# Linear attention and a feed-forward layer on one core: k read from its staging buffer, key-value products of two batches together, row squares summed through ScalarE's accumulator

## The chip, the cores and the metric

The kernel runs on one core of a Trainium2 chip. The metric is the device time of one execution in microseconds. Lower is better.

The core has a matrix engine (TensorE, "PE" in the profile; its weight loads are "PEld"), a vector engine (VectorE, "DVE"), an activation engine (ScalarE, "ACT"), GpSimd ("POOL") and SyncE ("SP"). Each works through its own instructions in order. Here POOL and SP do little but issue transfers (DMA).

## The reference

```python
kv  = einsum('bhsd,bhse->bhde', k, v)          # 8 batches, 8 heads, 576 rows, 64 columns
out = einsum('bhsd,bhde->bhse', q, kv)
rms = sqrt(mean(out * out, axis=-1) + 1e-06)   # over the 64 columns of a head
x   = out / rms * g_norm                       # then [4608 tokens, 512], heads side by side
h   = x @ w_in                                 # 512 -> 2048
g   = maximum(h, 0) + alpha * minimum(h, 0)
y   = g @ w_out                                # 2048 -> 512
```

The inputs and the result are float32; the kernel computes in fp16 and accumulates in float32.

## The kernel before

**Windows, stages, units.** The 4608 tokens are cut into nine windows of 512. Stage w does three things at once: the first feed-forward product of window w, the second product of window w-1, and the attention of window w+1, which makes the input of the next stage. A stage has 16 units (`u`). The instructions of every engine stand in the order in which the code writes them; there is no planner.

**A unit.** `m1_group(w, g)` runs four matmuls of 128x512 (L507) into a PSUM bank `h_ps`. From stage 2 on there are two such banks, taken in turn. ScalarE computes `m_sb` = relu(-h) from the bank (L514), and VectorE then `gt` = h + beta * m_sb (L518), after which the bank is free. Then come seven matmuls of 128x256 for the second product of the window before (L688). That product is done with seven block products instead of eight; the sums that this needs are VectorE's (`s_sum`, L623 to L629). Finished parts are read out by ScalarE (`p1` in unit 2, `c11` in unit 7) or by VectorE (`u2`, `u3`, `c22`, `c21`, `c12`) and stored by DMAs of POOL and SP. In unit 0 of stages 3 and up the first matmul group is split (`late`): 384 columns first, the last 128 columns after four of the seven other matmuls (L530), since these columns of the input are the last to arrive.

**Attention of windows 3 and up** ("rows" form, `attention(w + 1, u)`). `row_kv(b)` makes the key-value products of one batch, head by head: 40 matmuls of 64 columns (L1001) into a PSUM tile, two ScalarE copies from there into `kv_masked` (L1007). `rows_mm` makes the outputs of four blocks of 128 tokens (L452), token by row, eight heads of 64 columns next to each other. For each block i: `rows_sq` squares 512 columns on ScalarE (L463), `rows_ssq` sums each head's 64 squares on VectorE (L469), `rows_rs` makes the reciprocal root of eight numbers per row on ScalarE (L479), `rows_norm` multiplies on VectorE (L487) and has SP issue a DMA transpose of the block into `xt` (L492), the input of the next stage. `ROW_AT` says in which unit each step stands. From window 4 on: kv in unit 0, both `rows_mm` in unit 1, the squares of blocks 0 to 3 in units 1, 3, 5, 7, the sums in 2, 4, 7, 9, root and norm in 3, 6, 8, 11. Window 3 (`W_ROW`, handled in stage 2) has a schedule of its own, up to unit 12.

**Loads.** At the start of stage w, `load_gated(w + 2)` puts the loads of batch w+2 on POOL's queue: the last 64 rows of q, k, v (`load_rem`, into `qsb`, `ksb`, `vsb`) and the first 512 rows (`load_main` into the staging buffers `kst` and `vst`, two of each; `load_q` in four parts). POOL issues them in order, together with most stores; its first load of a stage waits for the last transpose of the q before. q is transposed by DMAs on SP's queue (`dma_t`). v is read where it was staged. k is first regrouped from `kst` (head, tile, column) into `ksb` (tile, head, column): for batches 4 to 7 by four ScalarE copies (`regroup_pair`, L195) in units 9, 11, 13 and 15 of stage w, for batch 3 by two ScalarE copies and one VectorE copy in unit 0 of stage 2. There are three `ksb`/`vsb` buffers (`NBUF`) and two `kv_masked` tiles.

Of the kernel before, what the change touches and what calls it, by code (L numbers as in the profile page):

```python
# [17 lines left out]
def kernel(  # L18
# [11 lines left out]
    nc = tc.nc  # L30
# [41 lines left out]
    def row_tile(shape, name):  # L72
        if not row_pool:
            early.close()
            row_pool.append(
                ctx.enter_context(tc.tile_pool(name="psr", bufs=2, space=bass.MemoryType.PSUM))
            )
        t = row_pool[0].tile([P, 2, W], FP32, name=name, tag="r")
        n = 1
        for x in shape:  # L80
            n *= x
        flat = t[:].rearrange("p b n -> p (b n)")[:, 0:n]
        names = [f"x{i}" for i in range(len(shape))]
        return flat.rearrange(
            f"p ({' '.join(names)}) -> p {' '.join(names)}", **dict(zip(names, shape))
        )
# [78 lines left out]
    def load_main(b, nm, h0=0, h1=H):  # L165
        if (b, nm) not in stages:
            stages[b, nm] = stage_p.tile([P, H, TPP, D], FP16, name=f"{nm}st", tag=f"{nm}st")
        nc.gpsimd.dma_start(
            out=stages[b, nm][:, h0:h1].rearrange("p h t d -> p h (t d)"),
            in_=srcs[nm][b, h0:h1, 0:MAIN, :].rearrange("h (p t) d -> p h (t d)", t=TPP),  # L170
        )
# [13 lines left out]
    def load_rem(b, nm):  # L185
        nc.gpsimd.dma_start(
            out=buf_of(b, nm)[0:REM, 0 if nm == "v" else TPP, :, :],
            in_=srcs[nm][b, :, MAIN:S, :].rearrange("h s d -> s h d"),
        )

    def regroup(b, nm, h0, h1, eng=None):
        dst = buf_of(b, nm)[:, 0:TPP, h0:h1, :].rearrange("p t h d -> p h t d")
        src = stages[b, nm][:, h0:h1, :, :]
        if eng is nc.scalar:
            nc.scalar.copy(out=dst, in_=src)  # L195
        else:
            (eng or nc.vector).tensor_copy(out=dst, in_=src)
# [6 lines left out]
    def load_gated(b):  # L204
        load_rem(b, "q")
        if b == B_NAT:
            load_q(b)
        load_rem(b, "k")
        load_main(b, "k")
        if b > B_NAT:  # L210
            load_q(b)
        load_rem(b, "v")
        load_main(b, "v")

    def regroup0(nm, j, n=1):
        i, h = divmod(2 * j, HH)
# [1 line left out]
            out=bufs[0][nm][0:P0, :, 2 * j : 2 * (j + n), :].rearrange("p t h d -> p h t d"),  # L218
            in_=stages[0, nm, i][0:P0, h : h + 2 * n],
        )  # L220

    def regroup_pair(b, nm, j):
        regroup(b, nm, 2 * j, 2 * j + 2, nc.scalar)


    WQ = 4
    w_in_sb = []
# [72 lines left out]


    qts, kvs, xts = {}, {}, {}
    kv_masked = [const_p.tile([P, NPAIR, P], FP16, name=f"kv_masked{i}") for i in range(2)]

    def rows(b):
        return P0 if b == 0 else P
# [60 lines left out]
    def step_kv(b, j, pool=(ps_s, "s")):  # L367
        ks, vs = pair_cols(b, "k", j), pair_cols(b, "v", j)
        kv_ps = pool[0].tile([P, P], FP32, name="kv_ps", tag=pool[1])
        for t in range(n_runs(b)):  # L370
            nc.tensor.matmul(  # L371
                out=kv_ps[:],
                lhsT=ks(t),
                rhs=vs(t),
                start=(t == 0),
                stop=(t == n_runs(b) - 1),
            )
        kvs[b, j] = kv_masked[b % 2][:, j, :]
        nc.vector.tensor_mul(out=kvs[b, j], in0=kv_ps[:], in1=mask32[:])


# [78 lines left out]
    def rows_sq(w, i):  # L460
        o_ps = ots.pop((w, "r", i))
        sq = attn_p.tile([P, 2, NPAIR, D], FP16, name="sq_sb")
        nc.scalar.activation(out=sq[:], in_=o_ps, func=AF.Square)  # L463
        ots[w, "r", i] = (o_ps, sq)

    def rows_ssq(w, i):
        o_ps, sq = ots.pop((w, "r", i))
        ssq = attn_p.tile([P, 2, NPAIR], FP32, name="ssq_r")
        nc.vector.tensor_reduce(  # L469
            out=ssq[:].rearrange("p h j -> p (h j)"),  # L470
            in_=sq[:].rearrange("p h j d -> p (h j) d"),
            axis=mybir.AxisListType.X, op=ALU.add,
        )
        ots[w, "r", i] = (o_ps, ssq)
# [516 lines left out]
            ATT_1.setdefault(at, []).append((what, j))  # L991
    ATT = {"t": step_t, "kv": step_kv, "ot": step_ot, "ssq": step_ssq}

    def row_kv(b):
        kv_ps = row_tile([NPAIR, D], "kv_ps")
        for j in range(NPAIR):
            ks, vs = pair_cols(b, "k", j), pair_cols(b, "v", j)
            for t in range(n_runs(b)):
                for i in range(2):
                    rows_i = slice(i * D, (i + 1) * D)  # L1000
                    nc.tensor.matmul(  # L1001
                        out=kv_ps[rows_i, j, :], lhsT=ks(t)[:, i, :], rhs=vs(t)[:, i, :],
                        start=(t == 0), stop=(t == n_runs(b) - 1), skip_group_check=True,
                    )
        for i in range(2):
            rows_i = slice(i * D, (i + 1) * D)
            nc.scalar.copy(out=kv_masked[b % 2][rows_i, :, rows_i], in_=kv_ps[rows_i, :, :])  # L1007
        for j in range(NPAIR):
            kvs[b, j] = kv_masked[b % 2][:, j, :]

    ATT_ROW = {}
    ROW_AT = {
        True: dict(
# [1 line left out]
            rs=(5, 7, 9, 12), norm=(5, 7, 9, 12),  # L1015
        ),
        False: dict(
            kv=(0,), mm=(1, None, 1, None), sq=(1, 3, 5, 7), ssq=(2, 4, 7, 9),
            rs=(3, 6, 8, 11), norm=(3, 6, 8, 11),
        ),  # L1020
    }
# [10 lines left out]
    def attention(w, u):  # L1032
        if W_ROW <= w < NW:
            for what, j in ATT_ROW[w == W_ROW].get(u, ()):
                if what != "kv":
                    ROWS[what](w, j)
                elif w < B:
                    row_kv(w)
            if w + 1 < B:
                dma_t(w + 1, QT_AT[w == W_ROW].get(u, ()))  # L1040
        elif w < NW:
            for what, j in (ATT_1 if w == 2 else ATT_AT).get(u, ()):
                if what == "t" and w >= B_NAT:
                    continue
                if w < B or what in ("ot", "ssq"):
                    if w == 2 and what in ("kv", "ssq"):
                        pool = Q_POOL if j % 2 == 0 else S_POOL
                        (step_kv if what == "kv" else step_ssq)(w, j, pool)
                    else:
                        ATT[what](w, j)  # L1050

    REG_AT = {9 + 2 * j: (("k", j),) for j in range(NPAIR)}

    Y3_AT = [(13, 13), (13, 13), (13, 13), (13, 14), (14, 14), (14, 15), (15, 15), (15, 15), (15, 15), (15, 15), (15, 15), (15, 15), (15, 15), (15, 15), (15, 16), (16, 16)]

    for w in range(1, NW):
        if w + 2 < B:
            load_gated(w + 2)
        for u in range(NF):
            if w >= W_ROW - 1 and u in R_FIRST:  # L1060
                y_read(w - 1, R_FIRST[u])
            late = w >= W_ROW and u == 0
            if late:
                h_ps = h_bank()
                m1_cols(h_ps, w, G_ORDER[u], 0, W - P)
            else:
                m1_group(w, G_ORDER[u])
            if w < 3 and (w, u) in ((1, NF - 1), (2, 0)):
                s_sum(1, w, 2)
            if w == W_ROW - 1:  # L1070
                scale_w_in(G_ORDER[u])
            if w > 1:
                unit_sums(w, u)
            if w == 1 and u == 1:
                regroup(2, "k", 0, H)
            if w == 2 and u == 0:
                h_tags[0] = ("h1", "h2")
                h_turn[0] = 0
            if w > 2 and u == 0 and not late:
                y_read(w - 2, "c12")  # L1080
            if w == 1:
                for i in range(*Y3_AT[u]):
                    y_mm(ys[3], 0, 3, i)
                    if i == NF - 1:
                        y_out(ys[3], 0, 3)
            else:
                for i in range(u * PER, (u + 1) * PER):
                    prod_mm(w - 1, *Y_LIST[i])
                    if late and i == 3:
                        m1_cols(h_ps, w, G_ORDER[u], W - P, W)  # L1090
                        y_read(w - 2, "c12")
                        m1_evac(h_ps, w, G_ORDER[u])
                for what in (R_ROW if w >= W_ROW - 1 else Y_READS).get(u, ()):
                    y_read(w - 1, what)
            attention(w + 1, u)
            if w == 1 and u == 12:
                dma_t(3, (3, 4, 0, 1, 2))
            if w == 1:
                for k in {5: (0,), 7: (1,)}.get(u, ()):
                    s_sum(1, 1, k)  # L1100
                    s_sum(1, 2, k)
            if w + 2 < B:
                for nm, j in REG_AT.get(u, ()) if w > 1 else ():
                    regroup_pair(w + 2, nm, j)
            if w == 2:
                if u == 0:
                    regroup_pair(3, "k", 0)
                    regroup_pair(3, "k", 1)
                    regroup(3, "k", HH, H)
    w = NW - 1  # L1110
    store_engines[0] = (nc.sync, nc.scalar)
    Y_READS[13] = Y_READS.pop(14)
# [54 lines left out]
```

## Time and profile before

| | us |
|---|---|
| median of 3 runs | 274.97 (273.76 to 275.08) |
| the profiled execution | 275.59 |
| its span, first to last instruction | 273.6 |

| engine | busy us | share of the span |
|---|---|---|
| PE | 266.3 | 97% |
| DVE | 227.9 | 83% |
| ACT | 155.9 | 57% |
| POOL | 86.2 | 32% |

Stage 2 begins at about 67 us in the trace, stage 3 at 94.5, stage 4 at 122, stage 5 at 149.8, stage 6 at 177; stage 8 ends at about 258, and what is left is the second product of the last window.

How to read it: a line of groups gives the line of code, the engine, the operation, what is written and read, the shapes and the count, then the busy time in us and the mean length of one in ns, then the engine's idle time before these instructions and what ended it. A timeline line gives the start and the length in us; the bracket at its end is the idle time of that engine just before. Matmuls are pipelined, so the lengths of successive ones overlap and their ends are modelled; the spacing of their starts is what counts. A DMA line gives the size in KB and the us from issue to landing. The engine that is busy all the time sets the end; the idle time of another one costs nothing by itself.

### The profile page before, as it was taken

The numbers are of one execution on the slowest core, as the hardware profiler recorded it, in microseconds if no ns is written. First come the engines' busy times: TensorE is split into PE (matmuls) and PEld (weight loads), VectorE is DVE, ScalarE is ACT, GpSimd is POOL, SyncE is SP. The second block draws the span as 40 slices with busy tenths as digits, with TensorE's granted clock in tenths as the row PEclk, the third lists the DMA queues.
The fourth block names the chain that finished last, engine by engine and source line by source line (L and its number), as shares of the span: only waits on it lengthen the run. The fifth ranks groups of instructions, "written<-read, shape, count | busy, mean of one in ns | idle before, by whom it ended". The sixth has DMA issues, their size and how long they took to land.

```text
span 273.6 us, 5687 instructions
## 1 busy us (share of the span) xinstructions
PE 266.3 (97%) x2181; PEld 170.8 (62%) x2181; DVE 227.9 (83%) x432; ACT 155.9 (57%) x294; POOL 86.2 (32%) x123
## 2 busy tenths in 40 slices
PE   7799999999999999999999999999999999999995
PEld 2364464555666766666666666666666666666794
DVE  6459938899889979997999799979998999877863
ACT  3267555879989865645565556555544553443210
POOL 8773462780733355226421551100110012000200
PEclk9799999999999999999999999999999999999999
DMA  8999999999999689966996699720222122201223
GB/s 161 196 200 199 197 202 189 220 112 162 137 164 180 99 129 149 170 153 113 155 167 147 112 156 164 151 89 19 77 60 77 22 77 60 77 1 41 77 79 116
DMA packets 87343, 34.56 MB, mean 126 GB/s; under 512 B 58884, under 2 KB 85652, under 8 KB 87316
## 3 DMA queue, kind: packets, MB, share of 16 engines
q0 software_dynamic: 58064, 24.35, 69.5%
q1 hardware_dynamic: 28212, 8.83, 17.1%
q10 hardware_dynamic: 1040, 1.02, 1.2%
q8 instruction: 17, 0.28, 0.4%
q14 instruction: 10, 0.08, 0.1%
HBM read 36.71 MB, written 9.44 MB: 169 GB/s over the span
## 4 chain that ended last, share of the span: by engine, by line
PE 95%; DMA 2%; DVE 1%; issue 0%; ACT 0%; POOLq 0%
PE h_ps L507 43%; PE yY L688 15%; PE yX L688 10%; PE yZ L688 10%; PE y L539 5%; DMA vst<-in_v_dram 2%; PE h_ps L530 2%; PE kv_ps L371 2%; PE or_ps L452 1%; PE kv_ps L1001 1%; PE ssq_ps L416 1%; PE qt_ps L327 1%; PE ot_ps L393 1%; PE yZ L683 1%; PE warm_ps L295 0%
## 5 line engine op out<-in xcount | busy, mean ns | idle before, releaser
L507 PE MATMUL h_ps<-xt,w_in_sb 128*128 128x512 f16 x544 | 136.9, 379 | 0.0
L514 ACT ACTIVATE m_sb<-h_ps 128x512 f32<-128x512 f32 x144 | 86.1, 599 | 78.1 <-PE h_ps L507 67.7
L518 DVE SCALAR_TENSOR_TENSOR gt<-m_sb,beta_sb,h_ps 128x512 f16<-128x512 f32 x144 | 106.2, 744 | 24.1 <-ACT m_sb L514 22.5
L507 PEld LDWEIGHTS <-w_in_sb 128*128 128x128 f16 x544 | 52.1, 98 | 40.0
L550 POOL DMA_DIRECT2D out_dram<-y_sb x36 | 22.6, 630 | 134.3 <-ACT y_sb L726 53.4
L688 PEld LDWEIGHTS <-s 128*128 128x128 f16 x496 | 48.5, 98 | 19.1
L688 PEld LDWEIGHTS <-gt 128*128 128x128 f16 x384 | 37.3, 98 | 14.0
L688 PE MATMUL yY<-wsum,s 128*128 128x256 f16 x256 | 36.3, 273 | 0.0
L688 PE MATMUL yX<-w_out_sb,gt 128*128 128x256 f16 x256 | 36.1, 273 | 0.0
L177 POOL DMA_DIRECT2D qst<-in_q_dram x20 | 17.7, 923 | 1.8 <-DMA vst<-in_v_dram 1.8
L688 PE MATMUL yY<-wsum,gt 128*128 128x256 f16 x128 | 17.6, 273 | 0.0
L688 PE MATMUL yZ<-wsum,s 128*128 128x256 f16 x120 | 16.7, 273 | 0.0
L688 PE MATMUL yZ<-w_out_sb,s 128*128 128x256 f16 x120 | 16.7, 273 | 0.0
L487 DVE TENSOR_TENSOR x_rows<-or_ps,rstd_r 128x512 f16<-128x512 f32 x24 | 16.4, 683 | 0.0
L469 DVE TENSOR_REDUCE ssq_r<-sq_sb 128x8 f32<-128x512 f16 x24 | 16.3, 678 | 0.0
L463 ACT ACTIVATE sq_sb<-or_ps 128x512 f16<-128x512 f32 x24 | 14.4, 599 | 2.6 <-PE or_ps L452 2.6
L539 PE MATMUL y<-w_out_sb,gt 128*128 128x512 f16 x64 | 15.8, 379 | 0.0
L625 DVE TENSOR_TENSOR s<-s,gt 128x512 f16<-128x512 f16 x32 | 13.5, 421 | 0.5
L623 DVE TENSOR_TENSOR s<-gt 128x512 f16<-128x512 f16 x32 | 13.4, 418 | 0.0
L629 DVE TENSOR_TENSOR s<-gt,s 128x512 f16<-128x512 f16 x32 | 13.2, 417 | 0.0
L627 DVE TENSOR_TENSOR s<-gt 128x512 f16<-128x512 f16 x32 | 13.0, 418 | 0.0
L720 DVE TENSOR_TENSOR u<-yY,p 128x512 f32<-128x512 f32 x16 | 10.9, 683 | 1.9 <-PE yY L688 1.7
(88 smaller groups left out, 249.9 us busy)
## 6 DMA issues: line engine op xcount, KB each, us to landing
out_dram<-y_sb POOLq DMA_DIRECT2D x16, 256.0 KB, 2.7
kst<-in_k_dram POOLq DMA_DIRECT2D x7, 512.0 KB, 7.9
vst<-in_v_dram POOLq DMA_DIRECT2D x6, 512.0 KB, 10.5
qst<-in_q_dram POOLq DMA_DIRECT2D x20, 128.0 KB, 8.0
w_out_sb<-in_moe_w_out_dram POOLq DMA_DIRECT2D x8, 256.0 KB, 11.7
out_dram<-y_sb SPq DMA_DIRECT2D x5, 256.0 KB, 2.2
w_in_sb<-in_moe_w_in_dram POOLq DMA_DIRECT2D x2, 512.0 KB, 10.0
qst<-in_q_dram POOLq DMA_DIRECT2D x2, 512.0 KB, 12.1
```

What stands on the lines that cost most here:

```text
L177: nc.gpsimd.dma_start(out=st[:, t, :, :], in_=srcs["q"][b, :, t * P : (t + 1) * P, :].rearrange("h p d -> p h d"),)
L463: nc.scalar.activation(out=sq[:], in_=o_ps, func=AF.Square)
L469: nc.vector.tensor_reduce(out=ssq[:].rearrange("p h j -> p (h j)"), in_=sq[:].rearrange("p h j d -> p (h j) d"), axis=mybir.AxisListType.X ...
L487: nc.vector.tensor_tensor(out=xr[:].rearrange("p j h d -> p h j d"), in0=o_ps, in1=rstd[:].unsqueeze(3).to_broadcast([P, 2, NPAIR, D]), op ...
L507: nc.tensor.matmul(out=h_ps[:], lhsT=w_in_blk(c, g), rhs=xts[w][:, c, :], start=(c == 0), stop=(c == NC - 1),)
L514: nc.scalar.activation(out=m_sb[:], in_=h_ps[:], func=AF.Relu, scale=-1.0)
L518: nc.vector.scalar_tensor_tensor(out=gts[w, i][:, r, :], in0=m_sb[:], scalar=beta_sb[:, g : g + 1], in1=h_ps[:], op0=ALU.mult, op1=ALU.add,)
L539: nc.tensor.matmul(out=y[:], lhsT=gt_cols(w, g, a * P, (a + 1) * P), rhs=w_out_blk(g), start=(g == 0), stop=(g == NF - 1),)
L550: engs[store_turn[0] % len(engs)].dma_start(out=dst, in_=src)
L623: nc.vector.tensor_add(out=t[:], in0=a21, in1=a22)
L625: nc.vector.tensor_sub(out=t[:], in0=sums[w, 1, k][:], in1=a11)
L688: nc.tensor.matmul(out=bank, lhsT=lhs, rhs=rhs, start=fresh, stop=(c == NK - 1), skip_group_check=True,)
```

## The change

- `load_gated`: the k and v of batches 5 and 7 are loaded one stage earlier, behind those of batches 4 and 6 and on the same queue. Stages 3 and 5 load only q. In stage 2 q still stands between k and v of batch 4.
- The regrouping of k is gone for batches 3 to 7. `row_kv` reads k from the staging buffer through `head_rows`, as it read v.
- `row_kv` takes a list of batches: 3 alone (stage 2, unit 2), 4 and 5 (stage 3, unit 0), 6 and 7 (stage 5, unit 0). The products of two batches share a PSUM tile, and each of the two copies moves 64x512 elements instead of 64x256.
- `kv_masked` becomes one tile with three places instead of two tiles.
- `rows_sq` from window 4 on: eight ScalarE instructions of 64 columns per block, each of which also gives the sum of its squares through `accum_out`. `rows_ssq` stands only in window 3's schedule. That is 20 blocks (windows 4 to 8, in stages 3 to 7).

```diff
     def load_gated(b):
         load_rem(b, "q")
         if b == B_NAT:
             load_q(b)
-        load_rem(b, "k")
-        load_main(b, "k")
+        first, *more = {3: (3,), 4: (4, 5), 6: (6, 7)}.get(b, (None,))
+        if first:
+            load_rem(b, "k")
+            load_main(b, "k")
         if b > B_NAT:
             load_q(b)
-        load_rem(b, "v")
-        load_main(b, "v")
+        if first:
+            load_rem(b, "v")
+            load_main(b, "v")
+        for c in more:
+            for nm in ("k", "v"):
+                load_rem(c, nm)
+                load_main(c, nm)
...
-    kv_masked = [const_p.tile([P, NPAIR, P], FP16, name=f"kv_masked{i}") for i in range(2)]
+    kv_masked = const_p.tile([P, NBUF, NPAIR, P], FP16, name="kv_masked")
...
     def rows_sq(w, i):
         o_ps = ots.pop((w, "r", i))
         sq = attn_p.tile([P, 2, NPAIR, D], FP16, name="sq_sb")
-        nc.scalar.activation(out=sq[:], in_=o_ps, func=AF.Square)
-        ots[w, "r", i] = (o_ps, sq)
+        if w == W_ROW:
+            nc.scalar.activation(out=sq[:], in_=o_ps, func=AF.Square)
+            ots[w, "r", i] = (o_ps, sq)
+            return
+        ssq = attn_p.tile([P, 2, NPAIR], FP32, name="ssq_r", bufs=4)
+        for h in range(2):
+            for j in range(NPAIR):
+                nc.scalar.activation(
+                    out=sq[:, h, j], in_=o_ps[:, h, j], func=AF.Square,
+                    accum_out=ssq[:, h, j : j + 1],
+                )
+        ots[w, "r", i] = (o_ps, ssq)
...
-    def row_kv(b):
-        kv_ps = row_tile([NPAIR, D], "kv_ps")
-        for j in range(NPAIR):
-            ks, vs = pair_cols(b, "k", j), pair_cols(b, "v", j)
-            for t in range(n_runs(b)):
...
+    def head_rows(b, nm, h, t):
+        if t < TPP:
+            return stages[b, nm][:, h, t, :]
+        return buf_of(b, nm)[:, t if nm == "k" else 0, h, :]
+
+    def row_kv(bs):
+        n = len(bs)
+        kv_ps = row_tile([n, NPAIR, D], "kv_ps")
+        for x, b in enumerate(bs):
+            for j in range(NPAIR):
+                for t in range(NT):
+                    for i in range(2):
+                        nc.tensor.matmul(
+                            out=kv_ps[i * D : (i + 1) * D, x, j, :],
+                            lhsT=head_rows(b, "k", 2 * j + i, t),
+                            rhs=head_rows(b, "v", 2 * j + i, t),
+                            start=(t == 0), stop=(t == NT - 1), skip_group_check=True,
+                        )
+                kvs[b, j] = kv_masked[:, b % NBUF, j, :]
+        b0 = bs[0] % NBUF
         for i in range(2):
...
+            part = slice(i * D, (i + 1) * D)
+            nc.scalar.copy(out=kv_masked[part, b0 : b0 + n, :, part], in_=kv_ps[part])
+
+    KV_OF = {3: (3,), 4: (4, 5), 6: (6, 7)}
...
         False: dict(
-            kv=(0,), mm=(1, None, 1, None), sq=(1, 3, 5, 7), ssq=(2, 4, 7, 9),
+            kv=(0,), mm=(1, None, 1, None), sq=(1, 3, 5, 7),
             rs=(3, 6, 8, 11), norm=(3, 6, 8, 11),
         ),
...
-            if w + 2 < B:
-                for nm, j in REG_AT.get(u, ()) if w > 1 else ():
-                    regroup_pair(w + 2, nm, j)
-            if w == 2:
-                if u == 0:
-                    regroup_pair(3, "k", 0)
-                    regroup_pair(3, "k", 1)
-                    regroup(3, "k", HH, H)
```

More of the change, by code (lines that the diff above doesn't have):

```diff
@@ L220, in regroup0 @@
         )
-    def regroup_pair(b, nm, j):
-        regroup(b, nm, 2 * j, 2 * j + 2, nc.scalar)
     WQ = 4
@@ L377, in step_kv @@
             )
-        kvs[b, j] = kv_masked[b % 2][:, j, :]
+        kvs[b, j] = kv_masked[:, b % NBUF, j, :]
         nc.vector.tensor_mul(out=kvs[b, j], in0=kv_ps[:], in1=mask32[:])
@@ L462, in rows_sq @@
         sq = attn_p.tile([P, 2, NPAIR, D], FP16, name="sq_sb")
-        nc.scalar.activation(out=sq[:], in_=o_ps, func=AF.Square)
-        ots[w, "r", i] = (o_ps, sq)
+        if w == W_ROW:
[10 more added lines that the diff above has]
+        ots[w, "r", i] = (o_ps, ssq)
     def rows_ssq(w, i):
         o_ps, sq = ots.pop((w, "r", i))
-        ssq = attn_p.tile([P, 2, NPAIR], FP32, name="ssq_r")
+        ssq = attn_p.tile([P, 2, NPAIR], FP32, name="ssq_r", bufs=4)
         nc.vector.tensor_reduce(
@@ L992 @@
     ATT = {"t": step_t, "kv": step_kv, "ot": step_ot, "ssq": step_ssq}
-    def row_kv(b):
-        kv_ps = row_tile([NPAIR, D], "kv_ps")
-        for j in range(NPAIR):
-            ks, vs = pair_cols(b, "k", j), pair_cols(b, "v", j)
-            for t in range(n_runs(b)):
[L999 to L1004, printed above, removed]
+    def head_rows(b, nm, h, t):
[15 more added lines that the diff above has]
+                        )
+                kvs[b, j] = kv_masked[:, b % NBUF, j, :]
+        b0 = bs[0] % NBUF
         for i in range(2):
[L1006 to L1009, printed above, removed]
+            part = slice(i * D, (i + 1) * D)
+            nc.scalar.copy(out=kv_masked[part, b0 : b0 + n, :, part], in_=kv_ps[part])
+    KV_OF = {3: (3,), 4: (4, 5), 6: (6, 7)}
     ATT_ROW = {}
@@ L1036, in attention @@
                     ROWS[what](w, j)
-                elif w < B:
-                    row_kv(w)
+                elif w in KV_OF:
+                    row_kv(KV_OF[w])
             if w + 1 < B:
@@ L1050, in attention @@
                         ATT[what](w, j)
-    REG_AT = {9 + 2 * j: (("k", j),) for j in range(NPAIR)}
     Y3_AT = [(13, 13), (13, 13), (13, 13), (13, 14), (14, 14), (14, 15), (15, 15), (15, 15), (15, 15), (15, 15), (15, 15), (15, 15), (15, 15), (15, 15), (15, 16), (16, 16)]
```

## The prediction

> **What bounds the kernel now.** I read the busy shares first, then the stages one by one, then the idle times in the list of groups, and last the ScalarE rows and the transfers of single stages.
>
> ```profile
> PE 266.3 (97%) x2181; PEld 170.8 (62%) x2181; DVE 227.9 (83%) x432; ACT 155.9 (57%) x294; POOL 86.2 (32%) x123
> 95.00:122.00 27.00, 27.00 (x250) 18.11 (x249) 24.29 (x45) 16.23 (x34) 10.84 (x15) 1.00 1.18 148
> 150.40:178.00 27.60, 27.60 (x254) 18.51 (x252) 24.76 (x46) 16.20 (x32) 9.54 (x13) 1.00 1.18 144
> 258.00:273.60 15.60, 12.27 (x129) 11.01 (x126) 8.58 (x21) 1.17 (x2) 0.63 (x1) 1.00 0.31 102
> ```
>
> The first line is the whole span; the others are stretches (length, then busy time of PE, PEld, DVE, ACT, POOL, then clock, DMA share, GB/s). In the stages that the change touches TensorE is busy in every microsecond (27.00 of 27.00) at full granted clock. So what is taken from ScalarE or VectorE cannot shorten them; only TensorE's own work can, and any new wait on TensorE is paid in full. The question is whether the change makes TensorE wait.
>
> ScalarE rows, from the groups (busy, mean ns of one) and from the timeline of stage w=3 (start, length):
>
> ```profile
> L195 ACT COPY ksb<-kst 128x512 f16<-128x512 f16 x18 | 10.9, 611 | 0.0
> L479 ACT ACTIVATE rstd_r<-ssq_r,eps_t 128x8 f32<-128x8 f32 x24 | 7.2, 298 | 0.6
> L400 ACT ACTIVATE sq_sb<-ot_ps 128x512 f16<-128x512 f32 x11 | 6.3, 595 | 9.0 <-PE ot_ps L393 8.9
> L400 ACT ACTIVATE sq_sb<-ot_ps 128x256 f16<-128x256 f32 x2 | 0.7, 382 | 0.0
> ...
> 99.15 0.60 ACT L463 ACTIVATE sq_sb<-or_ps 128x512 f16<-128x512 f32 x1 [0.51 <-PE or_ps L452]
> 100.34 0.60 ACT L514 ACTIVATE m_sb<-h_ps 128x512 f32<-128x512 f32 x1 [0.60 <-PE h_ps L507]
> 100.84 0.58 ACT L716 COPY p<-yX 128x512 f32<-128x512 f32 x1
> ...
> 115.48 0.29 ACT L479 ACTIVATE rstd_r<-ssq_r,eps_t 128x8 f32<-128x8 f32 x1
> 115.68 0.61 ACT L195 COPY ksb<-kst 128x512 f16<-128x512 f16 x1
> ```
>
> To see: the start of one instruction to the start of the next is 0.50 us for 512 columns (100.34 to 100.84) and 0.20 us for 8 (115.48 to 115.68); a column costs (595 - 382)/256 = 0.83 ns. ScalarE has idle gaps of 0.5 to 0.6 us before each m_sb.
>
> Hand-over from bank to bank, from the PE and DVE timelines of the same stage, and the transfers in stretches of the trace (KB each, us to landing):
>
> ```profile
> 99.27 1.04 PE L507 MATMUL h_ps<-xt,w_in_sb 128*128 128x512 f16 x4
> 100.91 1.03 PE L507 MATMUL h_ps<-xt,w_in_sb 128*128 128x512 f16 x4
> 100.97 0.75 DVE L518 SCALAR_TENSOR_TENSOR gt<-m_sb,beta_sb,h_ps 128x512 f16<-128x512 f32 x1 [0.89 <-ACT m_sb L514]
> ...
> vst<-in_v_dram POOLq DMA_DIRECT2D x1, 512.0 KB, 10.7
> xt<-x_rows SPq DMA_TRANSPOSE x3, 5.1
> xt<-x_rows SPq DMA_TRANSPOSE x1, 2.5
> ```
>
> To see: a unit lasts 1.63 us; its m_sb starts 1.07 after its matmuls start, gt 0.63 after m_sb. The v load issued at 76.57 lands 10.7 later. Transposes issued from 80 to 88, while loads fill the queue, land after 5.1 us; the one of 91.90, after the loads are done, in 2.5.
>
> **TensorE's own work.** Matmul counts do not change. A key-value group takes 96.12 to 96.96 = 0.84 us, of which 40 matmuls at 16 ns are 0.64, so 0.2 is the changeover. Five groups become three: -0.4 us.
>
> **What is removed elsewhere.** 18 copies of 0.61 us from ScalarE (two in unit 0 of w=2, sixteen in units 9 to 15), one DVE copy of 0.42 and 20 of 24 reduces of 0.68 from VectorE. TensorE waits for none of them now: 0.
>
> **The squares.** 20 blocks go from one instruction of 512 columns (0.50) to eight of 64. One of 64 costs 0.50 - 448 x 0.83 ns = 0.127 us from start to start. The price of getting the sum out of the accumulator is in no row. It could be nothing, or a second instruction per head: 0.07 if it costs what 512 columns cost without their columns, 0.20 by the 128x8 row's spacing, 0.30 by its whole length. I take 0.10: such a read has no columns and no operand tensor, so it stands nearest to the bare 0.07. Then a block takes B = 8 x 0.227 = 1.82 us; the ends are 1.0 and 3.4.
>
> The Trainium skill ("ScalarE: Activation LUTs", What ACT_TABLE_LOAD costs) has 186 ns + 0.833 per element for an ACTIVATE without pointer operands, and 93 ns of overlap: 146 ns here where the rows give 127. By the page B would be 1.97 and the sum below 281.2 us instead of 279.2; the rows decide.
>
> What is queued behind a block on ScalarE: the rs of an earlier block, the next unit's m_sb, and through them DVE's norm and gt. TensorE needs the bank two units (3.26 us) after it last began to fill it. Counted from the start of the unit, the next unit's bank must be free at 4.89:
> - Block 0 (unit 1) starts 0.12 before unit 2; then m_sb, gt (0.63 + 0.75) and a 0.05 hand-over: free at B + 1.31 of 3.26, so B may be 1.95.
> - Block 1 (unit 3): m_sb ends its slot at 1.57, block, rs 0.30, norm 0.60 in front of gt on DVE, gt 0.75: 3.29 + B, so 1.60.
> - Block 2 (unit 5): 2.99 + B, so 1.90.
> - Block 3 (unit 7): the c11 copy (0.50) goes first: 3.49 + B, so 1.40.
>
> At 1.82 the wait is 0.22 + 0.42 = 0.64 us per stage, and five stages (w = 3 to 7) have such blocks: +3.2 us. At 1.0 it is 0; at 2.62 (a read of 0.20) 0.67 + 1.02 + 0.72 + 1.22 = 3.63, +18; at 3.4, +34. In units 9 to 15 ScalarE has the removed copies' time to catch up.
>
> **The copies of kv.** Two of 64x512 instead of 64x256: 0.368 + 0.21 = 0.58 each, 1.16 together, done 1.2 us after the group; rows_mm comes one unit later (1.63). Covered; without that unit 0.4 per group. VectorE and ScalarE need nothing else from it.
>
> **The loads.** POOL issues four more DMAs in w=2 right after v of batch 4 (0.70 + 0.91 + 0.76 + 0.97 = 3.3 us, 77.5 to 80.9), ahead of its stores, which come at 82.85: no delay. The staging buffer of batch 3 is read by its key-value matmuls until 72.5, so POOL does not wait. q of batch 5 is no longer behind them. Between the landings of k (71.56 + 8.4) and v (87.3) 1088 KB landed in 7.3 us. The 1152 KB of k5 and v5 need 7.7 more: 95.0, against 96.97 when TensorE reaches batch 5. In time by 2 us. But the queue is now full until 95, and the last xt transpose, on SP's queue at 91.90, then lands in 5.1 instead of 2.5: 97.0, while unit 0 needs these columns at 95.56. TensorE waits 1.4 us; 0 at 2.5, 4.0 at the longest landing of such a transpose (7.7). In w=4 the same burst (batches 6 and 7, v6 lands at 142.9, v7 at 150.6, needed at 152.3) meets the transpose of 145.03: 150.1, needed at 150.85: 0 (1.2 at a landing of 7.1). In w=3 and w=5 the loads shrink; TensorE did not wait there. Taken: +1.4 (0 to 5).
>
> **Sum.** -0.4 + 3.2 + 1.4 = +4.2 us. The profiled execution took 275.59 (span 273.6, 2.0 around it), 0.6 above the median of the runs; on the median, 274.97 + 4.2 = 279.2 us.
>
> **Rivals.**
> 1. The read is dear. A read of 0.17 to 0.30 makes B 2.4 to 3.4, ScalarE is late at every block, and the five stages grow by 2.7 to 6.8 us each (4B - 6.85). For: the only small ScalarE row, 128x8, lasts 298 ns. Against: that row has columns and a bias tensor. At 0.20: 274.97 - 0.4 + 18 + 1.4 = 294.
> 2. Only the loads hurt: B stays under 1.4 and the transpose at the start of w=3 is late: 274.97 - 0.4 + 1.4 = 276.0, up to 279 with a 7.7 landing. For: ScalarE's gaps and 9.8 us of removed copies. Against: the copies lie in units 9 to 15, the blocks in 1 to 7.
> 3. Not slower: ScalarE's gaps hold the blocks. It decides at a read under 0.05 us (B under 1.4), with the transpose landing in 3.7 or less (91.90 to 95.56). Then 274.97 - 0.4 = 274.6, no change. For: 16 of 27 us busy in a stage. Against: in units 1 to 8 of w=3 its gaps add up to about 5 us, and four blocks add 4 x (B - 0.5), as much already at B = 1.8.
> A real gain would need a wait on TensorE that goes, and the stretches show none.
>
> **How the numbers follow.** Forecast 0.50 (its own range 276 to 289), rival 1 0.15, rival 2 0.13, rival 3 0.17; 0.05 for a gain from what the modelled ends of matmuls may hide. About 0.5% (1.4 us) is what this measurement can tell from no change. Slower: 0.50 + 0.15 + 0.09 of rival 2 = 0.74; same: 0.04 + 0.17 = 0.21; faster 0.05. The range goes from rival 3 with a little run-to-run spread, 274.3, to 292, which is reached at B = 2.5 (4B - 6.85 = 3.2 us per stage, five times); about 0.05 lies below and 0.10 above.
>
> **What would show it.** ScalarE rows of 128x64, some 160, with or without a second row each, and a block of 1.8 us in units 1, 3, 5, 7. TensorE idle in w = 3 to 7 before h_ps, released by DVE gt, most in units 6 and 10 (0.2 and 0.4). TensorE idle before the 128-column h_ps matmuls at the start of w=3, released by the transposes of xt. Three key-value groups. I am wrong if TensorE stays at 100% in those stages (the read is free), if the waits are several us per stage (it is dear), or if the longest wait is before the kv matmuls of the doubled groups (k5 or v5 is late).

## The result, and the profile after

The changed kernel took 290.92 us (median of 4 runs, 289.79 to 292.62) beside 275.02 us before: a ratio of 1.0598, 95% interval 1.0548 to 1.0647. It is slower by 15.9 us, where 4.2 were forecast. Ratios and intervals, here and below, leave out runs that lie more than 1.5% above the fastest of their kernel (one of four each with k and v ahead of q and with the transfers that nobody reads), while medians and ranges are of all runs. The profiled execution has a span of 289.5 us, 15.9 more than before.

The busy shares and the clock row of the page of the changed kernel:

```profile
PE 272.3 (94%) x2181; PEld 173.2 (60%) x2181; DVE 215.7 (74%) x411; ACT 166.1 (57%) x572; POOL 87.0 (30%) x123
...
PE   7899899999999299999996799999999999999995
...
PEclk9999999999999779999999589999999999999999
```

TensorE runs the same 2181 matmuls, but it is busy 6.0 us longer (272.3 against 266.3) and idle 9.9 us more. Both lie in two places: slices 14 and 15 and slices 22 to 24, the beginnings of stages 3 and 5. The clock row dips in the same places.

The same two places as stretches (length, then busy time of PE, PEld, DVE, ACT, POOL, then granted clock, DMA share, GB/s):

```profile
93.80:100.40 6.60, 1.25 (x8) 0.81 (x9) 2.34 (x5) 0.48 (x1) 1.21 (x2) 0.79 1.19 210
100.40:104.80 4.40, 4.36 (x91) 3.28 (x91) 0.75 (x1) 1.40 (x3) 1.57 (x2) 0.54 0.66 139
104.80:129.50 24.70, 24.64 (x195) 16.22 (x194) 19.23 (x35) 17.04 (x86) 5.06 (x8) 1.00 0.69 87
156.90:163.50 6.60, 2.32 (x8) 1.20 (x9) 2.33 (x5) 0.00 (x0) 0.62 (x1) 0.66 1.17 117
163.50:169.40 5.90, 5.86 (x95) 4.03 (x95) 0.75 (x1) 2.26 (x4) 1.02 (x2) 0.51 0.86 115
```

From 93.80 to 100.40 TensorE works 1.25 of 6.60 us. In the next 4.40 us it works all the time, at a clock of 0.54. The rest of the stage is full again, at full clock. Stage 5 shows the same: 2.32 of 6.60, then 5.9 us at 0.51. What it waits for stands in its timeline (the bracket is the idle time before):

```profile
95.29 0.81 PE L543 MATMUL h_ps<-xt,w_in_sb 128*128 128x384 f16 x4 [1.49 <-DMA xt<-x_rows]
100.44 0.58 PE L543 MATMUL h_ps<-xt,w_in_sb 128*128 128x128 f16 x4 [3.90 <-DMA xt<-x_rows]
129.55 0.81 PE L543 MATMUL h_ps<-xt,w_in_sb 128*128 128x384 f16 x4
159.12 1.46 PE L543 MATMUL h_ps<-xt,w_in_sb 128*128 128x384 f16 x4 [2.24 <-DMA xt<-x_rows]
163.54 0.59 PE L543 MATMUL h_ps<-xt,w_in_sb 128*128 128x128 f16 x4 [2.10 <-DMA xt<-x_rows]
```

Four waits, 9.7 us together, all for the DMA transposes that bring the input of the new stage. How long a matmul takes shows the clock as well: four of 384 columns last 0.81 us at 95.29, after a wait of 1.49 us, as they do at 129.55 without a wait, but 1.46 us at 159.12, after a wait of 2.24.

The same group at the start of stages 3 and 4 in the kernel before:

```profile
94.48 0.81 PE L530 MATMUL h_ps<-xt,w_in_sb 128*128 128x384 f16 x4
122.06 0.81 PE L530 MATMUL h_ps<-xt,w_in_sb 128*128 128x384 f16 x4
```

Stage 3 of the changed kernel lasts from 93.80 (where the last matmul of stage 2 ends) to 129.55, 35.75 us against 27.58 before; stage 5 lasts 36.63 against 27.58. Stages 4, 6 and 7 change by -0.4, -0.5 and +0.3.

The transfers of stages 2 and 4 of the changed kernel, by time of issue (KB each, us to landing): v of batch 5 (issued at 82.02), the xt transposes of 85.85 and 91.06, then v of batch 7 (144.02) and the transposes of 147.87 and 151.99.

```profile
vst<-in_v_dram POOLq DMA_DIRECT2D x1, 512.0 KB, 16.1
...
xt<-x_rows SPq DMA_TRANSPOSE x1, 9.3
xt<-x_rows SPq DMA_TRANSPOSE x1, 9.3
...
vst<-in_v_dram POOLq DMA_DIRECT2D x1, 512.0 KB, 19.2
...
xt<-x_rows SPq DMA_TRANSPOSE x1, 11.2
xt<-x_rows SPq DMA_TRANSPOSE x1, 11.5
```

The last transpose of stage 2, which landed 2.5 us after its issue before the change, now takes 9.3. That of stage 4 takes 11.5; before (issued at 145.03) it took 3.2:

```profile
xt<-x_rows SPq DMA_TRANSPOSE x1, 3.2
```

ScalarE's side, from the groups and from the timeline of stage 3:

```profile
L473 ACT ACTIVATE sq_sb<-or_ps 128x64 f16<-128x64 f32 x160 | 33.1, 247 | 2.8 <-PE or_ps L455 2.8
L473 ACT ACTIVATION_READ_ACCUMULATOR sq_sb<-or_ps 128x1 f32 x160 | 32.7, 234 | 0.0
...
106.31 0.22 ACT L473 ACTIVATE sq_sb<-or_ps 128x64 f16<-128x64 f32 x1 [0.51 <-PE or_ps L455]
106.44 0.20 ACT L473 ACTIVATION_READ_ACCUMULATOR sq_sb<-or_ps 128x1 f32 x1
106.53 0.21 ACT L473 ACTIVATE sq_sb<-or_ps 128x64 f16<-128x64 f32 x1
106.63 0.20 ACT L473 ACTIVATION_READ_ACCUMULATOR sq_sb<-or_ps 128x1 f32 x1
106.72 0.23 ACT L473 ACTIVATE sq_sb<-or_ps 128x64 f16<-128x64 f32 x1
...
107.90 0.65 ACT L527 ACTIVATE m_sb<-h_ps 128x512 f32<-128x512 f32 x1
```

The sum does cost a second instruction. From start to start a square of 64 columns takes 0.10 us and a read 0.095. A block lasts from 106.31 to 107.90: 1.59 us.

### The profile page after: what moved, and what is told of

Same layout as the page of the kernel before. It is cut to its first block, busy times and chain, and to the rows that moved or that the text cites. A ratio compares the mean times of both kernels' runs of the same rounds, so it can differ in the third digit from the quotient of the medians.

```text
span 289.5 us, 5944 instructions
## 1 busy us (share of the span) xinstructions
PE 272.3 (94%) x2181; PEld 173.2 (60%) x2181; DVE 215.7 (74%) x411; ACT 166.1 (57%) x572; POOL 87.0 (30%) x123
## 4 chain that ended last, share of the span: by engine, by line
PE 71%; DMA 17%; ACT 5%; DVE 3%; issue 2%; POOL 1%; DVEq 0%; ACTq 0%; POOLq 0%
PE h_ps L520 32%; PE yY L701 11%; PE yX L701 10%; DMA qst<-in_q_dram 7%; DMA xt<-x_rows 7%; PE yZ L701 6%; PE y L552 4%; ACT sq_sb L473 3%; DMA w_in_sb<-in_moe_w_in_dram 2%; PE kv_ps L1019 2%; ACT m_sb L527 2%; PE h_ps L543 2%; DVE gt L531 2%; PE or_ps L455 1%; ACT y_sb L739 1%
## 5 line engine op out<-in xcount | busy, mean ns | idle before, releaser
L527 ACT ACTIVATE m_sb<-h_ps 128x512 f32<-128x512 f32 x144 | 87.4, 608 | 82.3 <-PE h_ps L520 57.7
L701 PEld LDWEIGHTS <-gt 128*128 128x128 f16 x384 | 38.0, 100 | 14.9 <-issue 0.9
L701 PE MATMUL yX<-w_out_sb,gt 128*128 128x256 f16 x256 | 37.6, 280 | 0.0
L473 ACT ACTIVATE sq_sb<-or_ps 128x64 f16<-128x64 f32 x160 | 33.1, 247 | 2.8 <-PE or_ps L455 2.8
L473 ACT ACTIVATION_READ_ACCUMULATOR sq_sb<-or_ps 128x1 f32 x160 | 32.7, 234 | 0.0
L543 PE MATMUL h_ps<-xt,w_in_sb 128*128 128x384 f16 (+1 forms) x48 | 8.2, 302 | 9.7 <-DMA xt<-x_rows 9.7
L552 PE MATMUL y<-w_out_sb,gt 128*128 128x512 f16 x64 | 15.9, 379 | 0.0
L186 POOL DMA_DIRECT2D qsb<-in_q_dram x7 | 5.1, 728 | 28.1 <-DMA qt_sb<-qsb 23.5
L636 DVE TENSOR_TENSOR s<-gt 128x512 f16<-128x512 f16 x32 | 13.4, 418 | 0.0
## 6 DMA issues: line engine op xcount, KB each, us to landing
vst<-in_v_dram POOLq DMA_DIRECT2D x6, 512.0 KB, 11.2
```

What stands on the lines that cost most here:

```text
L473: nc.scalar.activation(out=sq[:, h, j], in_=o_ps[:, h, j], func=AF.Square, accum_out=ssq[:, h, j : j + 1],)
L527: nc.scalar.activation(out=m_sb[:], in_=h_ps[:], func=AF.Relu, scale=-1.0)
L543: nc.tensor.matmul(out=h_ps[:, c0:c1], lhsT=w_in_blk(c, g), rhs=xts[w][:, c, c0:c1], start=(c == 0), stop=(c == NC - 1), skip_group_check= ...
L552: nc.tensor.matmul(out=y[:], lhsT=gt_cols(w, g, a * P, (a + 1) * P), rhs=w_out_blk(g), start=(g == 0), stop=(g == NF - 1),)
L636: nc.vector.tensor_add(out=t[:], in0=a21, in1=a22)
L701: nc.tensor.matmul(out=bank, lhsT=lhs, rhs=rhs, start=fresh, stop=(c == NK - 1), skip_group_check=True,)
```

## The experiments

Theory 1: the added loads keep the load queue full while the transposes for the next stage are issued, and TensorE waits for these and then runs at half clock. Theory 2: ScalarE's longer blocks delay the norms and so the transposes. Theory 3: the doubled key-value group waits for its own second batch.

**The loads back in their own stages**

```diff
-        first, *more = {3: (3,), 4: (4, 5), 6: (6, 7)}.get(b, (None,))
...
+        load_rem(b, "k")
+        load_main(b, "k")
         if b > B_NAT:
             load_q(b)
+        load_rem(b, "v")
+        load_main(b, "v")
...
-    KV_OF = {3: (3,), 4: (4, 5), 6: (6, 7)}
+    KV_OF = {b: (b,) for b in range(3, B)}
```

> The changed kernel with the loads of batches 5 and 7 back in their own stages and one batch per key-value group; k is still read as loaded and the squares still use the accumulators. Theory 1 (the loads: two more tensors in stages 2 and 4 keep the load queue full into the next stage, and the xt transposes land late): no wait before the first matmuls of stages 3 and 5, full clock, about 275.2 us (0.2 to 0.5 over before from ScalarE's blocks). Theory 2 (the squares: ScalarE's blocks delay norms and transposes): stage 5 still waits about 4 us and runs at half clock after it, about 283 us. Theory 3 (the two-batch group waits for its own second batch): 275.2 too.

Measured: 276.3 us, ratio 1.0050 (1.0032 to 1.0069). From stage 2 on TensorE has no wait for a transfer. So the loads together with the grouping carry nearly all of the loss (what is left, 1.3 us, is what the squares cost alone, below), and theory 2 falls: the blocks are still there and stage 5 starts in time.

**The squares back as they were**

```diff
-        if w == W_ROW:
-            nc.scalar.activation(out=sq[:], in_=o_ps, func=AF.Square)
-            ots[w, "r", i] = (o_ps, sq)
-            return
+        nc.scalar.activation(out=sq[:], in_=o_ps, func=AF.Square)
+        ots[w, "r", i] = (o_ps, sq)
+        return
...
-            kv=(0,), mm=(1, None, 1, None), sq=(1, 3, 5, 7),
+            kv=(0,), mm=(1, None, 1, None), sq=(1, 3, 5, 7), ssq=(2, 4, 7, 9),
```

> The changed kernel with the squares as before: one ScalarE instruction of 512 columns per block and the sum on VectorE. Theory 1: nearly all of the loss stays, 290 to 291 us, transposes of stage 2 landing in 8 to 9.5 us. Theory 2: stage 5's wait goes, about 283 us. Theory 3: 290 to 291.

Measured: 286.42 us (285.4 to 289.65), ratio 1.0454 (1.0380 to 1.0527). The waits stay with the old squares:

```profile
97.85 0.81 PE L542 MATMUL h_ps<-xt,w_in_sb 128*128 128x384 f16 x4 [3.77 <-DMA xt<-x_rows]
159.03 0.58 PE L542 MATMUL h_ps<-xt,w_in_sb 128*128 128x128 f16 x4 [4.77 <-DMA xt<-x_rows]
```

Some 11.4 us are thus the loads' and the grouping's without the new squares. That is less than expected under theory 1: with the accumulators the loss was 15.9. The clock has a part in the difference. After the wait of 4.77 us it is 0.50, but after that of 3.77 us it stays at 1.00 (97.80 to 101.00; the four matmuls last 0.81 us, as at full clock), and TensorE's busy time is 268.5 us where the changed kernel has 272.3.

**Nothing but the squares**

```diff
-        nc.scalar.activation(out=sq[:], in_=o_ps, func=AF.Square)
-        ots[w, "r", i] = (o_ps, sq)
+        if w == W_ROW:
+            nc.scalar.activation(out=sq[:], in_=o_ps, func=AF.Square)
+            ots[w, "r", i] = (o_ps, sq)
+            return
+        ssq = attn_p.tile([P, 2, NPAIR], FP32, name="ssq_r", bufs=4)
+        for h in range(2):
+            for j in range(NPAIR):
+                nc.scalar.activation(
+                    out=sq[:, h, j], in_=o_ps[:, h, j], func=AF.Square,
+                    accum_out=ssq[:, h, j : j + 1],
+                )
+        ots[w, "r", i] = (o_ps, ssq)
...
-            kv=(0,), mm=(1, None, 1, None), sq=(1, 3, 5, 7), ssq=(2, 4, 7, 9),
+            kv=(0,), mm=(1, None, 1, None), sq=(1, 3, 5, 7),
```

> The kernel before with nothing but the squares changed to eight instructions with an accumulator. A block takes 8 x 0.195 = 1.56 us by the changed kernel's rows. The limits of my working (1.95, 1.60, 1.90, 1.40 us) leave a wait of 0.16 us per stage in unit 10. Theories 1 and 3: 275 to 276 us. Theory 2: 279 to 283 us.

Measured: 276.36 us, ratio 1.0053 (1.0033 to 1.0073). The timeline of TensorE, starts of units 4 to 11 of stage 3 in this run:

```profile
101.36 1.03 PE L517 MATMUL h_ps<-xt,w_in_sb 128*128 128x512 f16 x4
102.99 1.03 PE L517 MATMUL h_ps<-xt,w_in_sb 128*128 128x512 f16 x4
104.65 1.02 PE L517 MATMUL h_ps<-xt,w_in_sb 128*128 128x512 f16 x4
106.36 1.02 PE L517 MATMUL h_ps<-xt,w_in_sb 128*128 128x512 f16 x4
107.98 1.03 PE L517 MATMUL h_ps<-xt,w_in_sb 128*128 128x512 f16 x4
109.61 1.03 PE L517 MATMUL h_ps<-xt,w_in_sb 128*128 128x512 f16 x4
111.46 1.02 PE L517 MATMUL h_ps<-xt,w_in_sb 128*128 128x512 f16 x4
113.09 1.03 PE L517 MATMUL h_ps<-xt,w_in_sb 128*128 128x512 f16 x4
```

The starts are 1.63 us apart, but 106.36 comes 0.08 late and 111.46 (unit 10) 0.22 late. Unit 10 takes the bank of unit 8 (107.98), which VectorE gives free at 111.41, after a wait for ScalarE's `m_sb`:

```profile
110.66 0.75 DVE L528 SCALAR_TENSOR_TENSOR gt<-m_sb,beta_sb,h_ps 128x512 f16<-128x512 f32 x1 [1.18 <-ACT m_sb L524]
```

This is the chain of the prediction, behind block 3. The five stages with such blocks are 0.32 to 0.35 us longer than before (stage 3: 27.92 against 27.58), 1.7 us together; the medians differ by 1.4. VectorE is relieved by 12 us (215.8 busy) and nothing is gained by that.

**k read as loaded, and nothing else but `kv_masked` as one tile**

```diff
-            ks, vs = pair_cols(b, "k", j), pair_cols(b, "v", j)
...
+                            lhsT=head_rows(b, "k", 2 * j + i, t),
+                            rhs=head_rows(b, "v", 2 * j + i, t),
...
-                for nm, j in REG_AT.get(u, ()) if w > 1 else ():
-                    regroup_pair(w + 2, nm, j)
```

> The kernel before with one part of the change: k is read from the staging buffer, one batch per group, loads in their own stages, squares as before. The regrouping copies are gone. All theories: TensorE has no wait to lose, 275 us, the same as before.

Measured: 274.73 us, ratio 1.0013 (0.9999 to 1.0027). The removed copies bring nothing, as work off TensorE's path should.

**Transfers that nobody reads**

```diff
         load_rem(b, "v")
         load_main(b, "v")
+        if b in (4, 6):
+            for i, nm in enumerate(("k", "v")):
+                nc.gpsimd.dma_start(
+                    out=bufs[0]["q"][i * REM : (i + 1) * REM, TPP],
+                    in_=srcs[nm][b + 1, :, MAIN:S, :].rearrange("h s d -> s h d"),
+                )
+                nc.gpsimd.dma_start(
+                    out=bufs[1 + i]["k"][:, 0:TPP].rearrange("p t h d -> p (t h d)").rearrange(
+                        "p (h x) -> p h x", h=H
+                    ),
+                    in_=srcs[nm][b + 1, :, 0:MAIN, :].rearrange("h (p t) d -> p h (t d)", t=TPP),
+                )
```

> The kernel before with k read as loaded, the loads, groups and squares as before, and in stages 2 and 4, behind v, four more transfers of the sizes that the change adds there (k and v of the next batch, 1152 KB); nobody reads what they bring. Theory 1 (the queue is full and the transposes suffer): the waits before h_ps at the start of stages 3 and 5 appear, with half clock behind them, 286 to 291 us. Theory 3 (the two-batch group waits for its second batch): no wait, since nothing depends on these transfers, 275 us.

Measured: 288.94 us (284.83 to 290.22), ratio 1.0473 (1.0393 to 1.0554). The timeline of its profiled execution, the shortest of the four:

```profile
94.36 0.81 PE L548 MATMUL h_ps<-xt,w_in_sb 128*128 128x384 f16 x4 [1.20 <-DMA xt<-x_rows]
99.32 0.59 PE L548 MATMUL h_ps<-xt,w_in_sb 128*128 128x128 f16 x4 [3.71 <-DMA xt<-x_rows]
...
156.38 0.82 PE L548 MATMUL h_ps<-xt,w_in_sb 128*128 128x384 f16 x4 [0.73 <-DMA xt<-x_rows]
160.04 0.38 PE L548 MATMUL h_ps<-xt,w_in_sb 128*128 128x128 f16 x4 [2.39 <-DMA xt<-x_rows]
```

The waits are there although nothing depends on these transfers. (After the last of them, 2.39 us, the four matmuls last 0.38 us, as at full clock; after that of 3.71 us, 0.59.) Beside the run with k as loaded this is the one difference. Theory 1 holds, and theory 3 is not needed.

**Half of them**

```diff
-            for i, nm in enumerate(("k", "v")):
+            for i, nm in enumerate(("k",)):
```

> Half of the idle transfers: only k of the next batch (576 KB) behind v in stages 2 and 4; all else as in the run with the idle transfers. If what counts is whether the load queue is still full when the last xt transposes are issued (about 1.5 us of slack in stage 2, 2.8 in stage 4): the queue ends some 4 us later than in the kernel before, at about 91.5 us of the trace in stage 2, just when the last transpose is issued. A wait of 0 to 2 us at the start of stage 3, none at stage 5, 275 to 278 us. If every transfer costs in proportion: half of the loss, 281 to 282 us.

Measured: 275.38 us, ratio 1.0041 (1.0022 to 1.0061). From stage 2 on TensorE waits 0.63 us at the start of stage 3 and nowhere else. The added load lands at 90.7 in stage 2, just as the last transpose is issued (90.65); this one lands after 4.6 us. 576 KB more in each of two stages cost 0.9 us and 1152 KB cost 13 to 14: the price is not in proportion. By this run, the one before and the next, what counts is how much is still queued when the last transposes go out.

**The same transfers later in the stage**

```diff
             attention(w + 1, u)
+            if u == 13:
+                idle_loads(w + 2)
```

> All of the idle transfers, but issued by POOL in unit 13 of stages 2 and 4 (after the last xt transpose of the stage) and not at its start. If the loss comes from the coincidence of the burst with the xt transposes: no wait at the starts of stages 3 and 5, 275 to 276.5 us. If the amount that a stage has to move is what costs, or the next stage's transposes suffer as much: 280 us or more.

Measured: 281.29 us (279.04 to 282.7), ratio 1.0220 (1.0171 to 1.0268), in the second of the two ranges that were expected. The starts of stages 3 and 5 are free of waits, but that of stage 4 is not (and that of stage 6 has 0.7 us):

```profile
125.88 1.44 PE L550 MATMUL h_ps<-xt,w_in_sb 128*128 128x384 f16 x4 [4.44 <-DMA xt<-x_rows]
...
106.18 0.71 POOL L187 DMA_DIRECT2D qsb<-in_q_dram  x1 [10.83 <-DMA qt_sb<-qsb]
```

The second line says why. The late burst holds up the last transposes of q. POOL's next loads wait for these by the program, so they start at 106.18 (99.23 in the kernel before), and their queue is full when stage 3 issues its own xt transposes. The burst has been handed on by one stage.

**k and v ahead of q on POOL's queue**

```diff
+        first, *more = {3: (3,), 4: (4, 5), 6: (6, 7)}.get(b, (None,))
+        if first and b > B_NAT:
+            for nm in ("k", "v"):
+                load_rem(b, nm)
+                load_main(b, nm)
         load_rem(b, "q")
+        load_q(b)
         if b == B_NAT:
-            load_q(b)
...
+            for nm in ("k", "v"):
+                load_rem(b, nm)
+                load_main(b, nm)
         for c in more:
```

> The changed kernel with another order on POOL's queue at the start of stages 2 and 4: k and v of batch 4 (6) first, then q with its remainder, then k and v of batch 5 (7). Nothing else. POOL waits for the last transpose of the q before in front of the remainder of q, so k and v start before that wait and not behind it. Theory 1: the queue is empty several us before the next stage, the transposes land in 2.5 to 5 us, no wait, 275 us. Theory 2: about 283 us. Theory 3: k and v of batch 5 land earlier too, 275 us.

Measured: 285.09 us, ratio 1.0353 (1.0307 to 1.0400); 275 was expected. The groups of TensorE's waits, from 60 us on:

```profile
PE or_ps L454 <- DMA qt_sb<-qst: 4.7, 2, 3.5
PE h_ps L542 <- DMA xt<-x_rows: 0.9, 1, 0.9
```

The xt transposes of stage 2 now land in 2.5 to 2.8 us. But the loads that start earlier fall on the transposes of q for batch 3 (8.9 us to landing), which the first `rows_mm` of stage 2 needs. So the loss moved to another transpose. The same order with the old squares:

> The order of loads of the run with k and v first, and the squares as before on ScalarE and VectorE. Theory 1: 274.6 to 275 us; beside the run with accumulators the difference is the price of ScalarE's blocks, 0 to 0.8 us.

Its runs lie between 281.48 and 288.81 us (median 286.29), too wide to say anything of the squares; 275 was expected here too, for the same mistaken reason.

**Matmuls in the waits**

```diff
+    FILL = {3: (6, 65), 5: (10, 35)}
...
+            nc.tensor.matmul(
+                out=h_ps[:, c0:c1], lhsT=w_in_blk(0, 0), rhs=w_out_blk(0)[:, c0:c1],
+                start=True, stop=True, skip_group_check=True,
+            )
...
                 h_ps = h_bank()
+                fill(h_ps, FILL.get(w, (0, 0))[0], 0, W)
...
+                        fill(h_ps, FILL.get(w, (0, 0))[1], W - P, W)
```

> The changed kernel with filler matmuls (operands that are long there, results overwritten) in the two places of stages 3 and 5 where TensorE waits for xt: 6 of 512 columns and 65 of 128 in stage 3, 10 and 35 in stage 5, some 5 us and 4 us of work. They are to keep TensorE busy during the wait. If half of the rest of the loss is the clock that falls to 0.5 after the wait (6.8 and 10.2 us at 0.5 in the changed kernel, 6 us more of busy time): the clock stays at 1.0 and the time is 285 us. If the clock does not follow the idle time: 291 us or more.

Measured: 285.49 us, ratio 1.0385 (1.0345 to 1.0426), 5.4 us less than the changed kernel. The stretches around its two starts, and the last 128 columns of the first:

```profile
93.00:100.50 7.50, 6.99 (x90) 5.58 (x88) 2.92 (x6) 1.05 (x2) 1.21 (x2) 1.00 1.15 194
100.50:105.00 4.50, 4.50 (x131) 3.24 (x129) 1.52 (x3) 2.90 (x10) 2.22 (x3) 1.00 0.58 118
155.00:162.00 7.00, 5.41 (x57) 3.81 (x55) 2.41 (x5) 0.00 (x0) 0.70 (x1) 1.00 1.37 171
...
100.25 0.38 PE L543 MATMUL h_ps<-xt,w_in_sb 128*128 128x128 f16 x4 [0.18 <-DMA xt<-x_rows]
```

The clock stays at 1.00 and the last 128 columns still come no sooner (100.25; 100.44 in the changed kernel). So of the loss some 5 to 6 us are the clock after the wait, and 10 are the wait. The Trainium skill ("TensorE: Matmul & The Clock Gate", Part 1: The HAM clock gate) says that the clock is halved when the engine has been idle and comes back after sustained work. The rows of this case agree: 0.54 and 0.51 in the stretches that follow the waits and 1.00 behind them, and 1.00 throughout where the waits were filled. How long a wait has to be does not come out of these runs: 2.24 us was enough in the changed kernel, and 3.77 us was not with the old squares.

No run beat the kernel before.

## Why the prediction was wrong

The direction was right, and both costs that the sum named (late transposes of xt, ScalarE's blocks) are in the runs. But the forecast change was a quarter of the true one, and the fall of the clock was not in it. That 290.9 lies inside the range of 274.3 to 292 is luck: the upper end was worked out from blocks of 2.5 us, and the blocks took 1.59; the term that grew was the loads', which was allowed +5 at most. By its steps:

- **"TensorE waits 1.4 us ... Taken: +1.4 (0 to 5)"** is the step that failed. The forecast took 5.1 us for the landing of a transpose in a full queue, and 7.7 as the worst. Both rows came from stages with three tensors queued; with five, the landings were 9.3 us in stage 2 and 11.2 and 11.5 in stage 4. Only the last transpose was priced. The one before it was late as well, so each stage waited twice: 1.49 + 3.90 and 2.24 + 2.10, 9.7 us. The wait in stage 4's burst, put at 0 with 1.2 as its end, was 4.3.
- **The price of a wait.** "Any new wait on TensorE is paid in full" was too little. In the changed kernel the granted clock is 0.5 for the first work after the waits of both stages, and busy time rose by 6.0 us. No term of the sum held this; filling the waits took 5.4 us off. Not every wait had this price: in other runs 3.77 and 2.39 us left the clock at 1.00.
- **"In time by 2 us"**: v of batch 5 landed at 98.1 and not at 95.0, later than the 96.97 of the forecast. TensorE recorded no wait for it, since by then it stood waiting for xt. v of batch 4 landed at 87.3, as forecast, but k5 and v5 took 10.8 us after it where the earlier rate gave 7.7. "POOL does not wait" missed too: before the large k load it waited 0.84 us in stage 2 and 2.27 in stage 4.
- **The squares, +3.2.** Alone they cost 1.4 us (1.7 by the stages). The read was taken at 0.10 us and is 0.095; a square of 64 columns was taken at 0.127 and is 0.10. B is 1.59 and not 1.82. With it the limits give 0.19 us per stage, in unit 10 alone; measured were 0.34, 0.22 of them in unit 10. The estimate of 146 ns for 64 columns from the figures of the Trainium skill ("ScalarE: Activation LUTs", What ACT_TABLE_LOAD costs) was farther off than the rows' 127.
- **Removed copies and reduces, 0**: right for the copies (1.0013 for k as loaded, with an interval that holds 1). The reduces were taken out only together with the squares, so their part is not shown by itself.
- **TensorE's own work, -0.4**: right. Where the two-batch group runs at full clock (the run with matmuls in the waits), it takes 1.48 us (100.80 to 102.28) where two groups took 0.84 each: 0.2 less, twice.

Rival 1, a dear read, fell: the read costs 0.095. Its 294 us is near the measurement for a reason that did not hold. Rival 2 named the mechanism that decided, but its 276 to 279 went by the same landing times.

Two things stay open. The loads alone cost 11.4 us with the old squares and 13 to 14 as idle transfers, the squares alone 1.4, and both together 15.9. Between the profiled executions with and without the new squares lie 5.7 us, 3.8 of them TensorE's busy time, where the clock fell after one wait less. Whether the squares have a part in that, or the kernels with waits only scatter (their runs spread over 3 to 7 us, those of the others over 0.3 to 2.3), was not settled. And how the transposes come to be held up behind the loads was not tried: the runs show that they are, and with how much queued, not by which resource.

## What to carry to other kernels

When a transfer is moved earlier, look for who else has transfers in that stretch, and do not take the longest landing in the present trace for the worst: with more queued it grew here beyond all rows there were. In this kernel 576 KB more in each of two stages were nearly free and 1152 KB cost 5%. And where TensorE is busy all the time, a wait of some us can cost more than its length: here 9.9 us of idle time brought 6.0 us of slower work behind it.

## What the runs showed of the hardware

- ScalarE's accumulator is read by an instruction of its own, with a row of 234 ns but a spacing of 0.095 us from start to start.
- A DMA transpose of 128x512 that lands in 2.5 us on quiet queues took 9.3 to 11.5 in stages in which POOL queued five tensors of 576 KB.
- Transposes on SP's queue and loads on POOL's delayed each other in turn: a late burst held up the transposes of q, POOL's next loads wait for these by the program, and the wait came up a whole stage later (4.44 us in stage 4).
- TensorE's granted clock after a wait for a transfer was 0.50 in most cases (after 2.24, 3.71, 3.90, 4.44 and 4.77 us) and 1.00 in others (after 1.49, 2.39 and 3.77 us).
